# Outputs 4 to 7 of the first token pair by seven products, larger VectorE shares in that pair, and W1I of outputs 6 and 7 at place 15

## The chip, the cores and the metric

The kernel runs on one core of a Trainium2 chip. The metric is the device time of one execution in microseconds (us): 1032.77 us, the median of three runs (1032.61 to 1032.79). The engines are TensorE (PE; its weight loads are listed apart as PEld), VectorE (DVE), ScalarE (ACT), GpSimd (POOL) and SyncE (SP), which issues most DMAs.

## What is computed

An attention over channels is followed by two feed-forward layers, for N = 6016 tokens, C = 256 channels and FF = 2048 hidden units, all in float32:

```python
qn, kn = q / (norm(q, axis=1) + 1e-6), k / (norm(k, axis=1) + 1e-6)
a = softmax(kn.T @ qn / tau)                 # 256 x 256
x = v @ a                                    # tokens x 256
h = x @ w_in;  x = (h * sigmoid(1.702 * h)) @ w_out
h = x @ w2_in; out = (max(h, 0) + alpha * min(h, 0)) @ w2_out
```

## The kernel before

Precision: every float32 operand is kept as a high and a low half in a reduced type, and every product is three passes (high x high, high x low, low x high; `PASSES`, L41). One pass is one matmul of 128 x 128 weights with 512 columns of tokens. High halves are made by ScalarE (a copy), low halves by VectorE (a subtraction).

The attention is folded into the first layer: x @ w_in = v @ (a @ w_in), so a "W product" (`emit_w` L729, `emit_pair` L717) makes the weights WI from a and w_in, and ScalarE and VectorE put its high and low halves into WI. `emit_pair(4)` and `emit_pair(6)` each do it for two outputs, with 12 matmuls.

Tokens come in twelve chunks, and two chunks are a pair (`p`); a layer is `l`. The hidden units come in eight groups of 256, called outputs (`j`, 0 to 7), and FF tiles are 128 wide. For one output and one pair, the first matmul of a layer is a 2 x 2 by 2 x 2 block product (two channel halves, two FF tiles, two chunks).

- `direct` (L884) computes it as four blocks of two products each. It does so for the first `STRASSEN` outputs of the first pair.
- `quartet` (L906) computes it by seven products, for all others. It needs sums of the weight blocks (S2, S3, S4: `combine` L688, with steps "whole", four small sums, and the low half, and ScalarE's high half in between) and differences of the token blocks (T1 to T4: `prepare` L630). Its order on TensorE is A11, S1 x T1, A12 x B21, S2 x T2, S3 x T3, A22 x T4, S4 x B22. Between them stand the eight `outs.next()` of the output before: three matmuls each of the layer's second weights (WO) with the activated units, 24 in all. ScalarE copies the product of A11 into a second bank (L934), onto which A12 x B21 is added. Products S2 and S3 are copied by ScalarE (`copy`) and added by VectorE (`add` L849): u22 is the bank of S1 x T1 plus a copy, and S4 x B22 is then added onto that same bank for u12.

A unit is one activated 128 x 512 block: ScalarE does its activation and its high half, VectorE its low half (`low`, L878).

The order on every engine is written by the program at build time. VectorE's other work, whose results are needed later, is cut into steps of about 0.6 us, which `beside(time, ...)` (L750) issues between TensorE's products, up to a share `time` of step prices. There are two sources. `conv` (`Converter` L190) splits the weights w1i (pieces `ia[j]`) and w1o (`ob_[j]`) that have been loaded as 64-bit numbers: five steps ("shift", "power", "rest", "less", "low"), or, for j > 3, three steps, a sum that a DMA on POOL's queue does (`sent` L160), a copy by ScalarE and a split (L164). A piece is opened at the earliest three places after its load (`LOADING`), the copy of a landed sum is asked for three places after it was sent (`LANDING`), one per place. `bg` holds the steps of T1 to T4 and of the sums. What is due first is issued first; ties go to `conv`. ScalarE's part of a step waits in `put_off` and is issued at the start of a later `beside`. `finish` issues what is left of some steps, just before it is needed.

A place is one call of `beside` in pair 0: 0 to 4 x STRASSEN - 1 in `direct` (four per output), then three per quartet. `mid_way` (L1065) runs at each place of `direct` and issues W products and new steps by number of place. `FREE` (L31) and `FIRST` (L32) are the shares of quartets and of direct places.

Of the kernel before, what the change touches and what calls it, by code (L numbers as in the profile page):

```python
# [30 lines left out]
FREE = ((0.7, 2.8, 1.7), (0.0, 0.8, 0.8))  # L31
FIRST = 2.1  # L32
AHEAD = 2
QK_PARTS = [1, 3] + [4] * 9 + [2, 2, 2, 1]
TAIL = 12
LOADING = 3
LANDING = 3
STRASSEN = 6
ON_VECTOR = (4, 5, 6, 8)
# [20 lines left out]
def attention_then_two_ffns(ctx: ExitStack, tc: tile.TileContext, q, k, vT, tau, w1i, w1o, w2i, w2o, alpha, outT):  # L60
# [45 lines left out]
    class Convert:  # L106
# [4 lines left out]
        most = PIECE  # L111
# [78 lines left out]
    class Converter:  # L190


        STEPS = (("shift", 0.45), ("power", 0.45), ("rest", 0.63), ("less", 0.63), ("low", 0.63))
        ADDED = (("shift", 0.45), ("power", 0.45), ("rest", 0.63))

# [30 lines left out]
        def time(self, piece):  # L226
            if not piece or self.landed():
                return 0.63
            return self.list(piece)[self.at][1]
# [35 lines left out]
        def step(self):  # L265
# [5 lines left out]
            if not self.next() or self.landed():  # L271
                self.settle()
                return 0.63
            if not self.open:
# [34 lines left out]
        def due(self):  # L309
            return min(x.due for x in self.left())  # L310

# [19 lines left out]
    with tc.manual_schedule():  # L331
# [37 lines left out]
        LAST = 4 * STRASSEN  # L369
        PAIRS = {4: 13, 6: min(21, LAST - 2)}  # L370
        for j, x in ia.items():
# [258 lines left out]
        def prepare(l, p):  # L630
# [20 lines left out]
            def minus(nm, a, b):  # L651
# [4 lines left out]
                ("B11", B11), ("B21", B21), ("T1", None), ("T2", None), ("T3", None), ("T4", None), ("B22", B22))}  # L656
            D = 0.63
            early = [
# [18 lines left out]
            if (l, p) == (0, 0):  # L677
                def last():
                    ops["T4"] = operand()
                    tmp["T4"] = tmp["T2"]  # L680
                    minus("T4", B21, "T2")
                steps = [early[i] for i in (2, 3, 6, 7)] + [late[0], Step(D, None, last, hi["T4"])] + [late[i] for i in (4, 5)]
                for x, due in zip(steps, (4, 4, 4, 4, 3, 3, 3, 3)):
                    x.due = LAST - due
                return steps
            return early, late

        def combine(hi, lo, hi_s, lo_s):  # L688
# [20 lines left out]

            steps = [Step(0.63, None, whole, kind=1), Step(0.9, None, sums_, high, 1), Step(0.63, high, low, kind=1)]  # L710
            combining.append(steps)
# [172 lines left out]
        def direct(j, outs, mid_way):  # L884
# [3 lines left out]
            for i, (f, c) in enumerate((f, c) for f in range(2) for c in range(2)):  # L888
# [11 lines left out]
                mid_way(i)  # L900
                beside(FIRST, most=2 if (j, i) == (STRASSEN - 1, 3) else 3)
                u.low()
                units.append((f, c, u.pair))
            return Outs(0, 0, j, units)

        def quartet(l, p, j, outs, carry):  # L906
# [20 lines left out]
            ends = (l, p, j) == (1, NP - 1, NQ - 1)  # L927
            most = 1 if l else 2 if narrow else None
            u11, u22, u21, u12 = (Unit(l, 2 * j + f, c) for f, c in ((0, c0), (1, c1), (1, c0), (0, c1)))
            fork = (l, p, j) != (1, 0, 0)  # L930
            a, b = bank(), bank()
            product(a, j, A11, ops["B11"], n, True, True)
# [20 lines left out]
            if j != 1:  # L953
                beside(FREE[l][0], place=0, most=most)
            if fork:
# [11 lines left out]
            if before:  # L967
                b12.low()
            outs.next()
            product(a, j, S2, ops["T2"], n, False, True)  # L970
            u2 = copy(a)
# [5 lines left out]
            outs.next()  # L977
            beside(FREE[l][1], most=most)
            finish(late[:4])
            product(a, j, S3, ops["T3"], n, False, True)  # L980
            u3 = copy(a)
# [3 lines left out]
            evacuate()  # L985
            beside(FREE[l][2], most=most)
            finish(late)
            u22.act()
            product(a, j, A22, ops["T4"], n, False, True)
# [14 lines left out]
            return Outs(l, p, j, [(0, c0, u11.pair), (1, c1, u22.pair), (1, c0, u21.pair), (0, c1, u12.pair)])  # L1004

        operands[0, 0] = blocks
        conv.ahead = True
# [27 lines left out]
        small = [flat(G), Convert.pool.tile([P, T], F32, tag="top", name="second", bufs=3)]  # L1035
        sums0, pair1 = [], []
        outs, carry = None, []
# [21 lines left out]
        def combining_of(n):  # L1059
# [3 lines left out]
            bg.extend(combined[n])  # L1063

        def mid_way(i):  # L1065
            at = 4 * j + i
            if j < 3 and i == 1:
                if j == 0:
                    conv.need([ob_[0]])
                emit_w(j + 1)  # L1070
            for n, due in PAIRS.items():
                if at == due:
                    emit_pair(n)
                    for m in (n, n + 1):
                        if m >= STRASSEN:
                            combining_of(m)
            if j == 2 and i == 0:
                nc.sync.dma_start(alpha_sb, alpha)
            if at == LAST - 10:
                sums0.extend(prepare(0, 0))  # L1080
                bg.extend(sums0)
            if at == LAST - 2:
                combining_of(0)
            next_pair()

        for j in range(NQ):
            if j:
                conv.need([ob_[j - 1]])
            if j < STRASSEN:
                outs = direct(j, outs, mid_way)  # L1090
                continue
            finish(combined[j])
            finish(sums0)
            next_pair()
# [152 lines left out]
```

## Time and profile before

| | |
|---|---|
| median of three runs | 1032.77 us |
| the profiled execution | 1033.06 us |
| its span, first to last instruction | 1031.3 us |
| granted TensorE clock | 1.00 of full in the whole span |
| TensorE busy | 1025.7 us, 99% |
| VectorE busy | 750.5 us, 73% |
| ScalarE busy | 758.5 us, 74% |

A row of the timeline is: start, duration, engine, line, operation, tiles written <- tiles read, how many are merged, and in brackets the idle time of the engine before it and what ended it. A matmul's duration covers its way through the array; matmuls overlap, so their pace is read from their starts. Operations of VectorE and ScalarE overlap a little too: successors start about 0.5 to 0.6 us after one another.

### The profile page before, as it was taken

The page shows a single profiled execution, that of the slowest core. Times are in us where ns is not written, and L with a number is a line of the kernel's source. Part 1 is how long each engine was busy: PE and PEld are TensorE (multiplying, and loading weights), DVE is VectorE, ACT ScalarE, POOL GpSimd, SP SyncE. Part 2 cuts the span into 40 slices and gives each one's busy share as a digit, 9 for nine tenths or more (in the row PEclk, how much of TensorE's full clock was granted, in tenths as well). Part 3 has the DMA queues.
Part 4 walks back from the last instruction along what each step waited for, and adds up shares of the span by engine and source line. Part 5 has one row for each costly group of instructions (what it writes and reads, how often), then busy time and mean ns, then how long its engine had stood idle before and what let it go on. Part 6 is the DMA issues. An engine that isn't in the chain of part 4 may idle for free.

```text
span 1031.3 us, 12536 instructions
## 1 busy us (share of the span) xinstructions
PE 1025.7 (99%) x4634; PEld 865.4 (84%) x4634; DVE 750.5 (73%) x1226; ACT 758.5 (74%) x1273; POOL 38.4 (4%) x50
## 2 busy tenths in 40 slices
PE   9999999999999999999999999999999999999998
PEld 8888888888888888888998888888888888888997
DVE  4788888877778765445637877787877787877766
ACT  6787787778778766666767777777777777867776
POOL 4401000000000000000100000000000000000000
PEclk9999999999999999999999999999999999999999
DMA  9737222224325312003553001001001000000100
GB/s 356 266 106 178 65 74 70 98 80 168 114 89 179 113 41 77 1 1 132 196 168 113 1 21 62 1 21 62 1 21 62 1 18 25 36 0 1 41 1 36
DMA packets 32445, 79.72 MB, mean 77 GB/s; under 512 B 3200, under 2 KB 7808, under 8 KB 32384
## 3 DMA queue, kind: packets, MB, share of 16 engines
q1 hardware_dynamic: 28928, 65.29, 18.3%
q0 software_dynamic: 3456, 13.63, 4.6%
q8 instruction: 36, 0.59, 0.2%
q14 instruction: 25, 0.20, 0.1%
HBM read 52.96 MB, written 23.86 MB: 74 GB/s over the span
## 4 chain that ended last, share of the span: by engine, by line
PE 99%; DMA 0%; SPq 0%; ACT 0%; issue 0%
PE ps_o L814 50%; PE ps_h L785 44%; PE gram L433 4%; PE pw L567 1%; PE pw L723 1%; DMA qk<-in_k 0%; SPq L453 0%; PE nrm L510 0%; ACT s L831 0%; PE bc L532 0%; PE pt L555 0%
## 5 line engine op out<-in xcount | busy, mean ns | idle before, releaser
L814 PE MATMUL ps_o<-ghi,wo 128*128 128x512 f32 (+1 forms) x1536 | 561.0, 385 | 0.0
L785 PE MATMUL ps_h<-x,wi 128*128 128x512 f32 (+1 forms) x2034 | 548.1, 385 | 0.0
L785 PEld LDWEIGHTS ps_h<-x,wi 128*128 128x128 f32 x2034 | 381.2, 188 | 71.9 <-DVE wi L579 0.4
L814 PEld LDWEIGHTS ps_o<-ghi,wo 128*128 128x128 f32 x1536 | 288.4, 188 | 53.7
L814 PE MATMUL ps_o<-glo,wo 128*128 128x512 f32 (+1 forms) x768 | 296.1, 386 | 0.0
L851 DVE TENSOR_TENSOR g<-ps_h,s 128x512 f32<-128x512 f32 (+1 forms) x177 | 120.1, 679 | 103.9 <-PE ps_h L785 63.5
L880 DVE SCALAR_TENSOR_TENSOR glo<-g,sign_sb,ghi 128x512 fp32r<-128x512 f32 (+1 forms) x192 | 141.5, 737 | 55.4 <-ACT ghi L874 51.0
L923 ACT COPY s<-ps_h 128x512 f32<-128x512 f32 (+1 forms) x177 | 102.2, 577 | 106.4 <-PE ps_h L785 102.2
L882 DVE TENSOR_TENSOR glo<-g,ghi 128x512 fp32r<-128x512 f32 (+1 forms) x192 | 126.4, 677 | 65.9 <-ACT ghi L876 65.1
L814 PEld LDWEIGHTS ps_o<-glo,wo 128*128 128x128 f32 x768 | 144.2, 188 | 27.2 <-DVE glo L880 0.3
L874 ACT ACTIVATE ghi<-g,sign_sb 128x512 fp32r<-128x512 f32 (+1 forms) x192 | 137.2, 714 | 16.3 <-DVE g L870 10.9
L876 ACT CAST ghi<-g 128x512 fp32r<-128x512 f32 (+1 forms) x192 | 113.1, 612 | 3.4
L862 ACT ACTIVATE g<-ps_h 128x512 f32<-128x512 f32 (+1 forms) x108 | 63.3, 586 | 41.6 <-PE ps_h L785 41.1
L866 ACT ACTIVATE g<-g,sign_sb 128x512 f32<-128x512 f32 (+1 forms) x97 | 69.4, 716 | 29.2 <-DVE g L851 28.7
L870 DVE SCALAR_TENSOR_TENSOR g<-g,slope_sb 128x512 f32<-128x512 f32 (+1 forms) x97 | 71.6, 738 | 16.7 <-ACT g L866 16.6
L870 DVE SCALAR_TENSOR_TENSOR g<-ps_h,slope_sb,g 128x512 f32<-128x512 f32 (+1 forms) x95 | 69.7, 734 | 0.0
L934 ACT COPY ps_h<-ps_h 128x512 f32<-128x512 f32 (+1 forms) x89 | 50.2, 564 | 26.4 <-PE ps_h L785 26.1
L866 ACT ACTIVATE g<-ps_h,sign_sb 128x512 f32<-128x512 f32 (+1 forms) x95 | 64.3, 676 | 1.9 <-PE ps_h L785 0.2
L862 ACT ACTIVATE g<-g 128x512 f32<-128x512 f32 (+1 forms) x84 | 52.3, 622 | 13.8 <-DVE g L851 13.3
L433 PE MATMUL gram<-qk 128*128 128x256 f32 x156 | 34.3, 380 | 1.0 <-DMA qk<-in_k 1.0
L433 PEld LDWEIGHTS gram<-qk 128*128 128x128 f32 x156 | 29.4, 190 | 5.2 <-issue 1.4
L649 DVE TENSOR_TENSOR x<-t,x 128x512 fp32r<-128x512 f32 (+1 forms) x48 | 32.0, 674 | 0.0
(123 smaller groups left out, 493.5 us busy)
## 6 DMA issues: line engine op xcount, KB each, us to landing
wi<-w2i POOLq DMA_DIRECT2D x8, 896.0 KB, 4.9
xraw<-in_vT SPq DMA_DIRECT2D x10, 512.0 KB, 5.5
x<-ob SPq DMA_DIRECT2D x20, 256.0 KB, 2.9
xraw<-x SPq DMA_DIRECT2D x10, 512.0 KB, 3.7
out_T<-ob SPq DMA_DIRECT2D x20, 256.0 KB, 2.0
qk<-in_q SPq DMA_DIRECT2D x9, 512.0 KB, 10.3
qk<-in_k SPq DMA_DIRECT2D x9, 512.0 KB, 10.6
raw<-in_w1i SPq DMA_DIRECT2D x8, 512.0 KB, 5.0
```

What stands on the lines that cost most here:

```text
L433: nc.tensor.matmul(gram[m][:, :C], tiles[i][:, 1, r, m * P:(m + 1) * P], tiles[i][:, 0, r, :], start=(t == 0), stop=(t == R - 1))
L785: nc.tensor.matmul(ps[:, :n], WI[:, wq, a, blk], x[:, b, :n], start=(start and i == 0), stop=(stop and i == 2), skip_group_check=True)
L814: nc.tensor.matmul(acc_ps[c][d][:, :n], WO[:, j, a, f, d * P:(d + 1) * P], (hi, lo)[b][:, :n], start=(start and i == 0), stop=(stop and i ...
L851: nc.vector.tensor_tensor(self.src, ps[:, :self.n], s[:, :self.n], ALU.add)
L862: nc.scalar.activation(self.g, self.src, AF.Gelu_apprx_sigmoid)
L866: nc.scalar.activation(self.g, self.src, AF.Copy, scale=sign_sb[:, self.f])
L870: nc.vector.scalar_tensor_tensor(self.g, self.src, slope_sb[:, self.f], self.g, ALU.mult, ALU.max)
L874: nc.scalar.activation(self.hi, self.g, AF.Copy, scale=sign_sb[:, self.f])
L876: nc.scalar.copy(self.hi, self.g)
L880: nc.vector.scalar_tensor_tensor(self.lo, self.g, sign_sb[:, self.f], f32(self.hi), ALU.mult, ALU.subtract)
L882: nc.vector.tensor_tensor(self.lo, self.g, f32(self.hi), ALU.subtract)
L923: nc.scalar.copy(s[:, :n], ps[:, :n])
```

## The change

`STRASSEN` goes from 6 to 4, so outputs 4 and 5 of the first pair are quartets too. Their sums are combined within that pair instead of the next one. W1I of outputs 6 and 7 is multiplied at place 15 (before: 21), so w1i's pieces 6 and 7 are converted ahead of w1o's 3 and 4. T1 to T4 of the first pair are put on the list at place 7 (before: 14), and each is finished ahead of the product that needs it instead of all ahead of the first quartet. Shares grow: in quartets of this pair from 0.7, 2.8, 1.7 to 0.9, 3.1, 2.1, at three direct places by 0.5, after a pair's W product by 1.0. Step prices of 0.63 become 0.62. A piece of `conv` counts as due one place earlier, or four where a DMA does the sum.

```diff
+MORE = (0, 1), (1, 1), (2, 1)
-STRASSEN = 6
+STRASSEN = 4
...
         def due(self):
-            return min(x.due for x in self.left())
+            return min(x.due - (0 if x in self.flying else 4 if x.added else 1) for x in self.left())
...
         LAST = 4 * STRASSEN
-        PAIRS = {4: 13, 6: min(21, LAST - 2)}
+        PAIRS = {4: 13, 6: 15}
...
-                for x, due in zip(steps, (4, 4, 4, 4, 3, 3, 3, 3)):
-                    x.due = LAST - due
+                for x, due in zip(steps, (-1, 0, -1, 0, 1, 1, 1, 1)):
+                    x.due = LAST + due
...
-                beside(FIRST, most=2 if (j, i) == (STRASSEN - 1, 3) else 3)
+                beside(FIRST + (0.5 if (j, i) in MORE else 0), most=2 if (j, i) == (STRASSEN - 1, 3) else 3)
...
+        def operands_of(which):
+
+            finish([x for i, x in enumerate(sums0) if (0, 1, 0, 1, 2, 3, 2, 3)[i] <= which])
...
+            free = (0.9, 3.1, 2.1) if narrow else FREE[l]
...
+            if narrow:
+                operands_of(0)
...
-                beside(FREE[l][0], place=0, most=most)
+                beside(free[0], place=0, most=most)
...
+            if narrow:
+                operands_of(1)
             product(a, j, S2, ops["T2"], n, False, True)
...
-            beside(FREE[l][1], most=most)
+            beside(free[1], most=most)
             finish(late[:4])
+            if narrow:
+                operands_of(2)
             product(a, j, S3, ops["T3"], n, False, True)
...
-            beside(FREE[l][2], most=most)
+            beside(free[2], most=most)
             finish(late)
+            if narrow:
+                operands_of(3)
...
+        def pairs(at):
+            for n, due in PAIRS.items():
+                if at == due:
+                    emit_pair(n)
+                    spare[0] += 1.0
+                    for m in (n, n + 1):
+                        if m >= STRASSEN:
+                            combining_of(m)
+            if at == max(LAST - 1, PAIRS[6]):
+                combining_of(0)
...
-            if at == LAST - 10:
+            if at == 7:
                 sums0.extend(prepare(0, 0))
                 bg.extend(sums0)
-            if at == LAST - 2:
-                combining_of(0)
...
+            pairs(conv.now)
             finish(combined[j])
-            finish(sums0)
             next_pair()
             outs = quartet(0, 0, j, outs, carry)
```

(In `mid_way` the loop over `PAIRS` becomes a call of `pairs(at)`.)

## Rows read from the trace of the kernel before

**Rows 1.** The page: part 1 (busy time, share, instructions) and part 4 (the chain's shares).

```profile
PE 1025.7 (99%) x4634; PEld 865.4 (84%) x4634; DVE 750.5 (73%) x1226; ACT 758.5 (74%) x1273; POOL 38.4 (4%) x50
...
PE 99%; DMA 0%; SPq 0%; ACT 0%; issue 0%
```

**Rows 2.** TensorE's waits: who waited for whom, us in total, times, longest.

```profile
PE idle L391 <- POOL ones L384: 1.1, 1, 1.1
PE gram L433 <- DMA qk<-in_k: 1.0, 1, 1.0
```

**Rows 3.** TensorE's timeline at the W product of outputs 4 and 5.

```profile
88.21 0.62 PE L723 MATMUL pw<-wi_hi,eT_hi 128*128 128x512 f32 x2
...
90.94 0.85 PE L785 MATMUL ps_h<-x,wi 128*128 128x512 f32 x3
...
96.38 0.84 PE L785 MATMUL ps_h<-x,wi 128*128 128x512 f32 x3
```

**Rows 4.** Groups by line and form, TensorE: the full-width products of line 785.

```profile
L785 PE MATMUL ps_h<-x,wi 128*128 128x512 f32 x1698 | 464.8, 389 | 0.0
```

**Rows 5.** DMA issues: operation, count, size, median us to landing.

```profile
p<-top POOLq DMA_DIRECT2D x8, 256.0 KB, 4.9
```

**Rows 6.** Busy time in a stretch, of quartet 7: length, then PE, PEld, DVE, ACT, POOL.

```profile
131.20:141.40 10.20, 10.20 (x47) 8.45 (x46) 8.18 (x13) 7.26 (x14) 0.00 (x0) 1.00 0.00 0
```

**Rows 7.** VectorE's timeline behind the W product of outputs 4 and 5.

```profile
91.86 0.75 DVE L727 SCALAR_TENSOR_TENSOR wi<-pw,rs,wi 128x512 fp32r<-128x512 f32 x1 [0.62 <-ACT wi L726]
92.53 0.68 DVE L158 SCALAR_TENSOR_TENSOR p<-raw,p 128x512 f32<-128x512 uint32 x1
```

**Rows 8.** VectorE's timeline, the four sums of output 6.

```profile
117.87 0.29 DVE L699 TENSOR_TENSOR s<-t 128x128 f32<-128x128 f32 x1
...
118.61 0.28 DVE L702 TENSOR_TENSOR s<-t,s 128x128 f32<-128x128 f32 x1
```

**Rows 9.** ScalarE's timeline into the first quartet.

```profile
118.93 0.62 ACT L708 CAST wi<-s 128x512 fp32r<-128x512 f32 x1
...
121.56 1.14 ACT L645 CAST x<-xraw 128x512 fp32r<-128x512 f32 x2
122.60 0.58 ACT L934 COPY ps_h<-ps_h 128x512 f32<-128x512 f32 x1
```

**Rows 10.** TensorE's timeline, the first quartet (output 6): A11 and A12.

```profile
120.88 0.84 PE L785 MATMUL ps_h<-x,wi 128*128 128x512 f32 x3
...
123.60 0.84 PE L785 MATMUL ps_h<-x,wi 128*128 128x512 f32 x3
```

**Rows 11.** VectorE's timeline, pair 1, output 0.

```profile
146.16 0.69 DVE L882 TENSOR_TENSOR glo<-g,ghi 128x512 fp32r<-128x512 f32 x1 [1.51 <-ACT ghi L876]
146.77 0.68 DVE L649 TENSOR_TENSOR x<-t,x 128x512 fp32r<-128x512 f32 x1
...
149.64 0.68 DVE L851 TENSOR_TENSOR g<-ps_h,s 128x512 f32<-128x512 f32 x1
150.24 0.68 DVE L835 COPY ob<-ps_o 128x512 f32<-128x512 f32 x1
150.84 0.68 DVE L705 TENSOR_TENSOR wi<-s,wi 128x512 fp32r<-128x512 f32 x1
```

**Rows 12.** TensorE's timeline: S4 of quartet 7; S3 and A22 of pair 1, output 0.

```profile
140.60 1.52 PE L785 MATMUL ps_h<-x,wi 128*128 128x512 f32 x6
...
147.40 0.84 PE L785 MATMUL ps_h<-x,wi 128*128 128x512 f32 x3
...
149.44 0.84 PE L785 MATMUL ps_h<-x,wi 128*128 128x512 f32 x3
```

**Rows 13.** VectorE's timeline, quartet 7.

```profile
135.96 0.69 DVE L882 TENSOR_TENSOR glo<-g,ghi 128x512 fp32r<-128x512 f32 x1 [1.44 <-ACT ghi L876]
...
138.98 0.69 DVE L851 TENSOR_TENSOR g<-ps_h,second 128x512 f32<-128x512 f32 x1
...
141.48 0.69 DVE L851 TENSOR_TENSOR g<-ps_h,G 128x512 f32<-128x512 f32 x1 [0.49 <-PE ps_h L785]
```

More of the change, by code (lines that the diff above doesn't have):

```diff
@@ L190, in attention_then_two_ffns @@
     class Converter:
-        STEPS = (("shift", 0.45), ("power", 0.45), ("rest", 0.63), ("less", 0.63), ("low", 0.63))
-        ADDED = (("shift", 0.45), ("power", 0.45), ("rest", 0.63))
+        STEPS = (("shift", 0.45), ("power", 0.45), ("rest", 0.62), ("less", 0.62), ("low", 0.62))
+        ADDED = (("shift", 0.45), ("power", 0.45), ("rest", 0.62))
         def __init__(self):
@@ L227, in time @@
             if not piece or self.landed():
-                return 0.63
+                return 0.62
             return self.list(piece)[self.at][1]
@@ L272, in step @@
                 self.settle()
-                return 0.63
+                return 0.62
             if not self.open:
@@ L656, in prepare @@
                 ("B11", B11), ("B21", B21), ("T1", None), ("T2", None), ("T3", None), ("T4", None), ("B22", B22))}
-            D = 0.63
+            D = 0.62
             early = [
@@ L708, in high @@
                 nc.scalar.copy(hi_s(), box["s"])
-            steps = [Step(0.63, None, whole, kind=1), Step(0.9, None, sums_, high, 1), Step(0.63, high, low, kind=1)]
+            steps = [Step(0.62, None, whole, kind=1), Step(0.9, None, sums_, high, 1), Step(0.62, high, low, kind=1)]
             combining.append(steps)
@@ L1004, in quartet @@
             return Outs(l, p, j, [(0, c0, u11.pair), (1, c1, u22.pair), (1, c0, u21.pair), (0, c1, u12.pair)])
+        sums0 = []
         operands[0, 0] = blocks
@@ L1035, in attention_then_two_ffns @@
         small = [flat(G), Convert.pool.tile([P, T], F32, tag="top", name="second", bufs=3)]
-        sums0, pair1 = [], []
+        pair1 = []
         outs, carry = None, []
@@ L1070, in mid_way @@
                 emit_w(j + 1)
[L1071 to L1076, printed above, removed]
+                if j + 1 >= STRASSEN:
+                    combining_of(j + 1)
+            pairs(at)
             if j == 2 and i == 0:
                 nc.sync.dma_start(alpha_sb, alpha)
-            if at == LAST - 10:
+            if at == 7:
                 sums0.extend(prepare(0, 0))
                 bg.extend(sums0)
-            if at == LAST - 2:
-                combining_of(0)
             next_pair()
```

## The prediction

> **What bounds the kernel now.** I read the page's first and fourth part, then TensorE's waits, then TensorE's timeline around the code that changes. TensorE is busy for 99% of the span and the chain that ended last is TensorE for 99% [rows 1]. Its only waits are two at the very start, 1.1 and 1.0 us [rows 2]. A busy share says little of pipelined matmuls, so the pace is read from starts: from 90.94 to 96.38 us there are 24 matmuls of 512 columns, so 5.44 / 24 = 0.227 us each, back to back, and the twelve of pair 4's W product take 2.73 [rows 3]. So the kernel is the number of matmuls times 0.227 us; everything else is hidden. A change can win only by taking matmuls away, and loses whenever it makes one wait.
>
> The profiled execution took 1033.06 us (span 1031.3), 0.29 above the median of 1032.77. I work out differences in its span and put them on the median.
>
> **What is taken away.** Outputs 4 and 5 have been computed directly, 4 blocks x 2 products x 3 passes = 24 matmuls each; as quartets they take 7 x 3 = 21. That is 6 of the 1698 full-width ones of this line [rows 4]: 6 x 0.227 = 1.36 us, 0.13%. Nothing else of TensorE's count moves: W products, outs and W sums are only placed elsewhere. 1.36 us is the most that can be gained.
>
> The Trainium skill has two other prices for a matmul of 512 columns ("TensorE: Matmul & The Clock Gate", Back-to-back issue gap): about 216 ns alone and 131 ns in a stream with weight loads. By them the gain would be an estimated 1.29 or 0.79 us; the trace's 0.227 us, in just such a stream, decides.
>
> **What the plan then does.** I followed the planner's rules by hand, place by place (a place is 12 matmuls, 2.72 us), with the new shares, prices and due times. Tried on before, the same rules give the order that VectorE's rows show.
>
> Places 0 to 9: ia6 and ia7 (W1I of 6 and 7) now come ahead of ob3. ia4's last step of three falls at place 7, ia5's at 8, ia6's at 9, ia7's at 10. At 9, ia7's load is not three places old, so T1 and T2 of the first pair run there. Each landed sum is asked for three places later and one per place: ia4 is split at 10, ia5 at 11, ia6 at 13 and ia7 at 14. A sum on POOL's queue lands in 4.9 us [rows 5], under three places (8.2), so this costs nothing. Loads of W1I go ahead of W1O's on SP's queue, where only order changes.
>
> Place 13 (share 2.1 + 1.0): W product of 4 and 5, then split ia6, last step of ob3, three steps of ob4. Place 14 (2.1): split ia7, low T1, first step of sums 4 ("whole"); 0.24 is left, too little for the four sums (0.9). Place 15 (3.1): W product of 6 and 7, then the four sums of 4, low T2, T3, T4. The low half of sums 4 is left for `finish(combined[4])`, ahead of quartet 4.
>
> **Edits that cost nothing.** Outputs 4 and 5 as quartets bring ScalarE three copies each and VectorE two adds each; the quartet of output 7, which has them all, leaves ScalarE 2.9 us and VectorE 2.0 us idle of 10.20 [rows 6]. The larger shares add two steps per quartet, 1.2 us, which still fits into VectorE's 2.0. The cover is that idle time; where it's gone, the adds are late for TensorE, which is the last rival below. The second W product needs ia7's low half 0.45 us after its start: it starts at 90.94 + 5.44 = 96.38 [rows 3], so by 96.83. VectorE leaves the first W product at 92.53 [rows 7]; five steps (2.73), place 13's low (0.6) and the split (0.7) end at 96.5. It is hidden by 0.3 us; I put 0 and keep 0.5 for the range.
>
> **The first wait: quartet 4.** Set S = 96.38, the start of the second W product. VectorE's second half of it begins 3.65 us after the start and the next step 0.67 later (91.86 and 92.53 against 88.21) [rows 3, 7], so the sums of 4 begin at S + 4.32; they take 1.02 from the first start to the last end (117.87 to 118.61 + 0.28) [rows 8]: S + 5.34. ScalarE's high half of them is issued ahead of quartet 4's copy of the first product into the second bank (L934). ScalarE goes in order, so the copy waits behind it: high half 0.62 [rows 9], but successors start about 0.5 after a predecessor, so copy from S + 5.9 to S + 6.5. Before, that copy has nothing late ahead of it: at 122.60 it ends 0.4 before its user at 123.60 [rows 9, 10]. The user, A12 x B21, adds onto that bank, and stands 2.72 us behind the quartet's start (120.88 to 123.60) [rows 10], so at S + 2.73 + 2.72 = S + 5.45 if nothing waits. It waits 1.1 us. Behind it S2 x T2 wants the low half of sums 4 in its third pass: VectorE does low T2, T3, T4, place 15's low (4 x 0.6) and then this one, ending at S + 8.4; TensorE, 1.1 late, would want it at S + 8.4 less a weight load. Another 0.3. T3's low half comes 0.1 late behind that. Together 1.5 us, bounds 1.0 (copy alone, faster hand-over) and 2.0.
>
> Quartets 4 to 7: by the same rules the second share of 3.1 takes four steps of 0.62, not five, since 3.1 less four times 0.62 is a hair under 0.62 in floating point. Counted through: the last steps are low T2, split ob7 and T3 of pair 1. So T4 (two steps) of pair 1 is still open when pair 1 begins; before, only three low halves are.
>
> **The second wait: pair 1, output 0.** The share of 0.7 takes T4's first step, the next one T4's second, T3's low half and two steps of sums 1. T4's high half can only be put on ScalarE at the third share, so T4's low half follows there, behind u22's add and the evacuation: those start at 149.64 and 150.24, and the next step at 150.84 [rows 11], so T4's low ends at 151.5. A22 x T4 starts at 149.44 and wants it in its second pass, at 149.67 [rows 12]. Also T3's low now follows T4's second step (146.77 + 0.6 to 148.06) where S3 x T3 wants it at 147.63; this is inside the same wait. Together 151.5 - 149.67 + 0.06 = 1.9 us, bounds 1.4 and 2.4 (VectorE's u11 low, for which it waits on ScalarE until 146.16 [rows 11], is the fixed point from which it counts).
>
> **Sum.** -1.36 + 0 + 1.5 + 1.9 = +2.0 us: 1034.8. Its own range is 1033.8 to 1036.0.
>
> **The rivals.**
> One: T4 is ready (a step more is done in quartets 4 to 7, such as a fifth in one second share). Then there is only the first wait: -1.36 + 1.5 = +0.1, 1032.9. For it: one step more anywhere in 30 is enough. Against: the four shares leave 0.24 to 0.79 unused and nothing of 0.62 that isn't waiting fits.
> Two: neither wait, as the sums of 4 get in at place 14, or the copy isn't behind them: 1031.4. For it: VectorE has idle time all over pair 0 (2.0 us of quartet 7) [rows 6]. Against: at S the sums stand behind a W product whose end is fixed.
> Three, on the far side: VectorE's larger shares make u22's add late in each of quartets 4 to 7. S4 adds into the bank that u22 reads. In quartet 7 the add starts at 138.98 with four steps ahead of it [rows 13] and S4 at 140.60 [rows 12]; a fifth step makes it 139.6, done at 140.3, still 0.3 early. From there on it costs: where the share holds six, or the sums (1.02 us for a price of 0.9), it is about 0.6 a quartet, 2.4 us in all, on top of the two waits: 1037.2. Against: VectorE idles 1.44 us ahead of u11's low and 0.49 ahead of u12's add [rows 13], so a late quartet recovers in the next.
> That the change doesn't take the products away can't be: their number is fixed by the code.
>
> **How the numbers follow.** Both waits 0.42, first alone 0.20, neither 0.22, VectorE late as well 0.12; 0.04 for what I don't see. Predicted 1034.8. The range holds the first three: 1031.2 (no wait, 0.2 under) to 1036.1. About 0.2%, 2.07 us, is what a measurement of this kernel can tell from no change. Faster by that isn't reachable (1.36): 0.02. Both waits lie just at the upper bound (+2.0 against 2.07), so somewhat under half of them, 0.19, is slower, with 0.12 and 0.02 from the others: 0.33. Same: 0.65.
>
> **What would show it.** The count of 512-column matmuls of L785 falls by 6. Right: two gaps in TensorE's starts, one in quartet 4 ahead of A12 x B21, with ScalarE's high half of sums 4 and L934 just ahead of it, and one in pair 1's output 0 ahead of the second matmul of A22 x T4. A gap ahead of the second W product's third matmul would show ia7 late; gaps ahead of S4 in quartets 5 to 7 the third rival. A TensorE timeline without a gap, or a first wait under 0.8 us, proves the walk through the plan wrong.

## The result, and the profile after

The changed kernel takes 1038.9 us, the median of six runs (1038.09 to 1040.96), against 1032.78 of the kernel before (six runs, 1032.61 to 1032.94): a ratio of 1.0062, 95% interval 1.0052 to 1.0072. It is slower, by 6.1 us. The forecast was 1034.8 with a range of 1031.2 to 1036.1, so the time lies outside the range. The profiled execution took 1040.96 us with a span of 1038.9, 7.6 us longer than that of before. Ranges and ratios below leave out one run of five_direct, which took 1284.99 us at a mean granted clock of 0.753.

Page of the kernel after: part 1, the granted clock in 40 slices, part 4. The chain was 99% TensorE before [rows 1]; now VectorE and ScalarE stand in it.

```profile
PE 1029.9 (99%) x4628; PEld 866.0 (83%) x4628; DVE 751.8 (72%) x1230; ACT 761.7 (73%) x1279; POOL 38.3 (4%) x50
...
PEclk9999899999999999999999999999999999999999
...
PE 94%; DVE 3%; ACT 1%; DMA 1%; issue 0%; SPq 0%; DVEq 0%
```

The count fell from 4634 to 4628: the six matmuls are gone. The 99% busy share tells nothing, as before. TensorE's waits of the kernel after (line waited for, total, times, longest); none of these three was there before [rows 2]:

```profile
PE ps_h L786 <- ACT wi L709: 1.8, 1, 1.8
PE ps_h L786 <- DVE wi L706: 1.6, 1, 1.6
...
PE pw L724 <- ACT wi_hi L152: 0.6, 1, 0.6
```

TensorE's timeline of the kernel after, around the two W products and quartet 4. Waits are read from starts: where the next matmul starts more than 0.227 us after the last, the rest is lost. It answers [rows 3] and [rows 10].

```profile
87.56 0.39 PE L815 MATMUL ps_o<-ghi,wo 128*128 128x512 f32 x1
88.53 0.73 PE L724 MATMUL pw<-wi_hi,eT_hi 128*128 128x512 f32 x2 [0.58 <-ACT wi_hi L152]
...
97.11 0.62 PE L724 MATMUL pw<-wi_hi,eT_hi 128*128 128x512 f32 x2
...
99.84 0.85 PE L786 MATMUL ps_h<-x,wi 128*128 128x512 f32 x3
...
100.98 0.39 PE L815 MATMUL ps_o<-ghi,wo 128*128 128x512 f32 x1
103.16 0.73 PE L786 MATMUL ps_h<-x,wi 128*128 128x512 f32 x2 [1.78 <-ACT wi L709]
105.52 0.80 PE L786 MATMUL ps_h<-x,wi 128*128 128x512 f32 x1 [1.63 <-DVE wi L706]
106.11 0.63 PE L815 MATMUL ps_o<-ghi,wo 128*128 128x512 f32 x1
106.53 0.63 PE L815 MATMUL ps_o<-glo,wo 128*128 128x512 f32 x1
```

Three things are to be seen.

- **The first W product** should start at 87.79 and starts at 88.53: 0.74, and 0.38 more within it.
- **Quartet 4**: A11 starts at 99.84. The second product, S1 x T1, should start at 101.21 and starts at 103.16, 1.95 late. Its third pass, which takes the low half of the sums, should start 0.45 behind that and starts at 105.52, another 1.91. Together 3.85 (the last digits of the three starts make the 0.01).
- **Then the matmuls are slow**: 0.43 us from start to start instead of 0.227, until 111.5: 14 matmuls in 6 us, 2.9 lost.

Stretches of the kernel after: length, then busy time of PE, PEld, DVE, ACT, POOL with their counts, the granted clock, DMA share and GB/s. Between quartet 4's two waits TensorE is busy for 0.90 of 4.30 us, the granted clock is 0.91, and in the six microseconds that follow it is 0.50: TensorE's lower level, 1.2 GHz. By the 0.91 the clock fell some 0.8 us before the second wait ended (4.30 x 0.09 / 0.5).

```profile
97.00:101.20 4.20, 4.20 (x20) 3.27 (x18) 3.25 (x6) 2.23 (x4) 0.52 (x1) 1.00 0.81 191
101.20:105.50 4.30, 0.90 (x3) 0.30 (x2) 4.26 (x11) 2.32 (x4) 0.00 (x0) 0.91 0.15 22
105.50:111.50 6.00, 5.99 (x14) 4.74 (x15) 2.04 (x5) 1.25 (x3) 0.00 (x0) 0.50 0.42 159
```

VectorE is busy for 4.26 of the 4.30 us in which TensorE mostly stands still. Its timeline shows with what: it begins the second half of the second W product at 100.77, makes the four sums of output 4 (101.44 to 102.45), then T2's low half, the differences T3 and T4, the low half of an activated unit, and only then the low half of the sums, which it ends at 105.46.

```profile
100.77 0.75 DVE L728 SCALAR_TENSOR_TENSOR wi<-pw,rs,wi 128x512 fp32r<-128x512 f32 x1 [0.62 <-ACT wi L727]
101.44 0.28 DVE L700 TENSOR_TENSOR s<-t 128x128 f32<-128x128 f32 x1
...
102.17 0.28 DVE L703 TENSOR_TENSOR s<-t,s 128x128 f32<-128x128 f32 x1
102.37 0.68 DVE L650 TENSOR_TENSOR x<-t,x 128x512 fp32r<-128x512 f32 x1
...
104.78 0.68 DVE L706 TENSOR_TENSOR wi<-s,wi 128x512 fp32r<-128x512 f32 x1
```

ScalarE's timeline: ia5's copy (L152 at 87.87), for which the first W product waits, stands behind a copy of w1o's and behind a scaling that waits for its load; in quartet 4 the high half of the sums (102.48) can only follow VectorE's last sum, and the copy of A11 into the second bank (now L942) follows it at once.

```profile
86.48 0.62 ACT L152 CAST wo<-top 128x512 fp32r<-128x512 f32 x1
87.31 0.66 ACT L139 ACTIVATE p<-raw 128x512 f32<-128x512 f32 x1 [0.21 <-DMA raw<-in_w1o]
87.87 0.61 ACT L152 CAST wi_hi<-p 128x512 fp32r<-128x512 f32 x1
...
102.48 0.62 ACT L709 CAST wi<-s 128x512 fp32r<-128x512 f32 x1 [1.75 <-DVE s L703]
103.01 0.58 ACT L942 COPY ps_h<-ps_h 128x512 f32<-128x512 f32 x1
```

The rest is five short waits: 0.06 in S1 x T1 of quartet 5, and four of 0.29 to 0.33 us ahead of S4 x B22, such as this one in the first pair, where VectorE's add of u22 starts behind the four small sums. TensorE's timeline, then VectorE's:

```profile
136.43 0.39 PE L815 MATMUL ps_o<-ghi,wo 128*128 128x512 f32 x1
136.84 1.65 PE L786 MATMUL ps_h<-x,wi 128*128 128x512 f32 x6
```

```profile
135.90 0.28 DVE L703 TENSOR_TENSOR s<-t,s 128x128 f32<-128x128 f32 x1
136.10 0.68 DVE L852 TENSOR_TENSOR g<-ps_h,second 128x512 f32<-128x512 f32 x1
```

The account of the two profiled spans (1038.88 and 1031.30, a difference of 7.59), every wait being the distance of two starts less 0.227:

| | us |
|---|---|
| six matmuls fewer | -1.36 |
| the stretch ahead of the first matmul of L786 (49.92 against 50.34) | -0.41 |
| wait at the first W product | 1.12 |
| quartet 4: S1 x T1, then its third pass | 3.85 |
| 14 matmuls at the lower clock | 2.92 |
| five short waits | 1.26 |
| sum | 7.38 |

The 0.2 that is missing is spread over distances too small to single out.

### The profile page after: what moved, and what is told of

It is laid out like the page before. It is cut to its first block, busy times and chain, and to the rows that moved or that the text cites. A ratio compares the mean times of both kernels' runs of the same rounds, so it can differ in the third digit from the quotient of the medians.

```text
span 1038.9 us, 12534 instructions
## 1 busy us (share of the span) xinstructions
PE 1029.9 (99%) x4628; PEld 866.0 (83%) x4628; DVE 751.8 (72%) x1230; ACT 761.7 (73%) x1279; POOL 38.3 (4%) x50
## 4 chain that ended last, share of the span: by engine, by line
PE 94%; DVE 3%; ACT 1%; DMA 1%; issue 0%; SPq 0%; DVEq 0%
PE ps_o L815 47%; PE ps_h L786 41%; PE gram L434 4%; DMA raw<-in_w1o 1%; PE pw L724 1%; DMA qk<-in_k 0%; DVE glo L883 0%; DVE p L159 0%; DVE t L654 0%; ACT g L863 0%; ACT ghi L877 0%; DVE x L650 0%; DVE top L183 0%; PE pw L568 0%; DVE p L156 0%
## 5 line engine op out<-in xcount | busy, mean ns | idle before, releaser
L786 PE MATMUL ps_h<-x,wi 128*128 128x512 f32 (+1 forms) x2028 | 548.8, 387 | 3.5 <-ACT wi L709 1.8
L786 PEld LDWEIGHTS ps_h<-x,wi 128*128 128x128 f32 x2028 | 380.7, 188 | 77.9 <-DVE wi L706 2.3
L863 ACT ACTIVATE g<-ps_h 128x512 f32<-128x512 f32 (+1 forms) x104 | 60.7, 584 | 32.7 <-PE ps_h L786 31.7
L942 ACT COPY ps_h<-ps_h 128x512 f32<-128x512 f32 (+1 forms) x91 | 51.3, 564 | 26.5 <-PE ps_h L786 26.3
L863 ACT ACTIVATE g<-g 128x512 f32<-128x512 f32 (+1 forms) x88 | 54.9, 624 | 17.6 <-DVE g L852 17.3
```

Of the source, the lines that this page charges most:

```text
L786: nc.tensor.matmul(ps[:, :n], WI[:, wq, a, blk], x[:, b, :n], start=(start and i == 0), stop=(stop and i == 2), skip_group_check=True)
L863: nc.scalar.activation(self.g, self.src, AF.Gelu_apprx_sigmoid)
```

## The experiments

Two theories are tested. One: the second W product at place 15 stands directly ahead of quartet 4 and, with the conversion of ia6 and ia7 ahead of it, leaves VectorE no time for what quartet 4 needs. Two: single steps stand in the wrong place, so that each wait can be taken away by itself. Two was the theory of the first four runs; one took this form only behind them. A third was the rival of the prediction that VectorE's larger shares make TensorE's operands late. Times below are medians with the range of the runs; ratios are to the kernel before on the same chip. "Waits" is the sum over the profiled execution, taken from TensorE's starts as above.

**sums4_first.** The sums of output 4 come ahead of ia6 and ia7 in the list.

```diff
-            x.due = PAIRS[j - j % 2] if j > 3 else 4 * j - 3
+            x.due = PAIRS[j - j % 2] - j // 6 if j > 3 else 4 * j - 3
...
+            if n == STRASSEN:
+                for x, due in zip(combined[n], (13, 13, 14)):
+                    x.due = due
```

> The changed kernel with one thing else: the sums of output 4 are due at 13 and 14 (ahead of w1o's pieces), and W1I of 6 and 7 one place earlier, so that VectorE and ScalarE make the sums at places 13 and 14 instead of behind the second W product. My theory: the waits of quartet 4 (3.85 us ahead of and in S1 x T1) go to under 0.3, no stretch at half clock follows (2.9 us in the profiled run), and the wait of the first W product for the copy of ia5 (1.1 us) stays; so some 6.7 us less than the profiled run of the changed kernel, 4 to 5 less than its median: 1034 to 1035 us. Rival (VectorE is overloaded in the whole of pair 0, and the wait only moves): a wait of 2 us or more stands somewhere else in quartets 4 and 5, and the time stays above 1037.

Measured: 1040.88 us (1040.6 to 1041.98), ratio 1.0080 (1.0065 to 1.0095). The sums are there in time, and the lower clock is gone, but 1.88 us stay in quartet 4, now for T1's low half (the 1.6 of the first row), and waits of 0.3 to 2.0 us stand at seven places behind it: 8.8 us in all. TensorE's waits, three of nine rows:

```profile
PE ps_h L786 <- DVE x L650: 2.5, 3, 1.6
PE ps_h L786 <- ACT wi L709: 1.0, 1, 1.0
PE ps_h L786 <- DVE g L852: 0.6, 1, 0.6
```

So the wait is not a matter of that one step: another is late in its place, behind the second W product and two steps of w1o's conversion.

**ia5_copy_early.** Four put-off steps instead of three at the place where ia5's sum is due to be copied, so that the first W product doesn't wait.

```diff
-  most=2 if (j, i) == (STRASSEN - 1, 3) else 3)
+  most=2 if (j, i) == (STRASSEN - 1, 3) else 4 if (j, i) == (2, 2) else 3)
```

> The changed kernel with one thing else: at place 10 ScalarE may issue four put-off items instead of three, so the copy of ia4 is issued there and the copy of ia5 one place earlier. My theory: the wait of 1.1 us ahead of and in the W product of 4 and 5 goes, everything else stays (waits of 3.8 us in quartet 4, the clock's drop): 1.1 us less than the changed kernel on the same chip, about 1037.5. Rival (the copy waits for the DMA that sums, not for its place in the order): the wait stays at 0.7 or more and the time is that of the changed kernel.

Measured: 1042.44 us (1041.51 to 1043.03), ratio 1.0093 (1.0078 to 1.0108). The wait at the first W product goes, and the second W product waits 2.5 us for ia7's low half instead; quartet 4 still waits, 3.0 us by TensorE's starts against 3.85:

```profile
PE pw L724 <- DVE wi_lo L166: 2.5, 1, 2.5
PE ps_h L786 <- DVE wi L706: 1.6, 1, 1.6
PE ps_h L786 <- ACT wi L709: 1.0, 1, 1.0
```

VectorE does not lack time here: it stands idle for 3.15 us ahead of ia6's split. ScalarE's copy of ia6 now comes while the first W product still reads the pair's tile, of which there is one (`wi_tiles`), and waits for its end at 90.7. VectorE's timeline, then ScalarE's:

```profile
91.58 0.69 DVE L166 TENSOR_TENSOR wi_lo<-p,wi_hi 128x512 fp32r<-128x512 f32 x1 [3.15 <-ACT wi_hi L152]
```

```profile
90.92 0.62 ACT L152 CAST wi_hi<-p 128x512 fp32r<-128x512 f32 x1 [1.89 <-PE pw L724]
```

The lower clock is part of this time too: the granted clock is 0.50 from 101.0 to 104.0, behind the second W product's wait, and from 107.8 to 111.0, behind those of quartet 4.

**both_waits_off.** The two edits together.

> Both edits of the two runs before. My theory: the two waits and the half clock are all that costs; left are 1.36 us gained by six matmuls less and about 1.3 us of four or five short waits (0.3 each) ahead of S4 x B22: 1032.7, within 0.1% of the kernel before. Rival (VectorE overloaded): 1035 or more, with a wait of over 1 us in quartets 4 to 7.

Measured: 1043.6 us (1042.71 to 1044.64), ratio 1.0108 (1.0091 to 1.0125), waits 11.0 us: 3.1 at the second W product, 1.9 in quartet 4, 6.0 at seven places up to 293 us. The 3.1 comes again of 3.16 us in which VectorE stands idle for ia6's copy. Theory two falls for these two edits: runs with a mean granted clock of 0.999 or more take 1038.1 to 1038.3 us for the changed kernel, 1040.6 to 1042.0 for sums4_first and 1042.7 to 1042.8 here (these two on another chip, where the kernel before takes 0.2 us more than beside as_changed). Whether VectorE lacks time or the order of its steps is at fault isn't told apart by them.

**old_shares.** The changed kernel with the shares of before in the first pair's quartets.

```diff
-            free = (0.9, 3.1, 2.1) if narrow else FREE[l]
+            free = FREE[l]
```

> The changed kernel with the quartets' shares of before (0.7, 2.8, 1.7). Theory: the waits of quartet 4 and of the first W product stay, since they are made ahead of these shares; the short waits ahead of S4 in quartets 5 to 7 (0.06, 0.29 and 0.33 us) go or move: within 0.8 us of the changed kernel on the same chip. Rival (the larger shares are what makes VectorE late): 3 us or more faster than the changed kernel.

Measured: 1047.37 us (1046.97 to 1047.89), ratio 1.0141 (1.0126 to 1.0156), waits 15.0 us, 1.6 of them at the lower clock behind quartet 4's. The larger shares don't cause the loss, they hold it down, by 7.2 us against as_changed on the same chip; that it would be within 0.8 was wrong too.

**before_new_shares.** The other side of it: the kernel before, with the larger shares.

> The kernel before with one part of the change alone: the larger shares (0.9, 3.1, 2.1) in the two quartets of its first pair. Theory: with prices of 0.63 the second share still holds four steps of 0.63 and a shift; nothing waits, or one wait of 0.3 ahead of S4: 1032.6 to 1033.2, the same as before. Rival (larger shares make u22's add late as such): two waits and more, 0.6 us or over.

Measured: 1033.03 us (1032.66 to 1033.52), ratio 1.0002 (0.9993 to 1.0011), one wait of 0.08. By themselves, in two quartets and at prices of 0.63, they cost nothing that can be measured.

**wait_filled.** The changed kernel with 16 more matmuls, whose result is overwritten, ahead of S1 x T1 in quartet 4: 3.6 us of work put into the 3.85 that TensorE waits there.

```diff
             d = bank()
+            if narrow and j == STRASSEN:
+                for _ in range(16):
+                    nc.tensor.matmul(d[:, :n], WI[:, j, 0, A11], ops["B11"][:, 0, :n], start=True, stop=True, skip_group_check=True)
             product(d, j, S1, ops["T1"], n, True, True)
```

> The changed kernel with 16 matmuls of 512 columns more, ahead of S1 x T1 of quartet 4, into the bank that this product then overwrites (they change nothing that is computed; 16 x 0.227 = 3.6 us, just the length of the wait). My theory: the half clock behind the wait comes of TensorE standing still; filled, the granted clock stays 1.00 all through and the time falls by what the half clock cost, to 1037.9 to 1038.2 on any chip, although 16 matmuls more are done. Rival (the clock falls for another reason, or the time lost is all the wait): a stretch at 0.50 remains and the time is 1038.5 or more.

Measured: 1038.21 us (1037.85 to 1038.42), ratio 1.0052 (1.0037 to 1.0067). Sixteen matmuls more, and not slower. The mean granted clock of its four runs is 0.999 to 1.000. Stretches of this kernel, the same as above, now with work in the first of them; the granted clock stays at 1.00:

```profile
101.20:105.50 4.30, 4.24 (x19) 3.19 (x18) 4.23 (x11) 2.33 (x4) 0.00 (x0) 1.00 0.23 55
105.50:111.50 6.00, 6.00 (x28) 4.87 (x27) 3.54 (x7) 3.90 (x7) 0.00 (x0) 1.00 0.36 138
```

**as_changed.** The changed kernel itself, once more, on another chip.

> The changed kernel itself, beside the others on the same chip. It ran in 1038.1 to 1041.0 us with a granted clock of 0.997 to 0.999. Theory: its waits are fixed by the order of instructions and don't vary; what varies is how long the half clock holds behind the wait in quartet 4 (0 to 3 us). Rival: the waits themselves vary from chip to chip, which the profile would show.

Measured: 1040.17 us (1038.31 to 1040.23), ratio 1.0071 (1.0054 to 1.0088). The profiled execution is the one of 1038.31. It has waits in the same places (6.5 us, 3.96 of them in quartet 4; 0.93 at the first W product, 0.45 in S1 x T1 of quartet 5) and no lower clock behind them:

```profile
101.00:105.30 4.30, 0.89 (x4) 0.33 (x3) 4.27 (x11) 2.33 (x4) 0.00 (x0) 1.00 0.16 24
105.30:111.30 6.00, 6.00 (x26) 4.90 (x27) 3.51 (x7) 3.59 (x7) 0.00 (x0) 1.00 0.43 161
```

So the waits are nearly the same in both, as an order fixed at build time lets expect, and what the clock adds is 2.9 us in one profiled execution and nothing in the other. Of the ten runs of this kernel, the four with a mean granted clock of 0.999 took 1038.1 to 1038.3 us, the six at 0.997 and 0.998 took 1039.5 to 1041.0. The six runs after the change spread over 2.87 us (1038.09 to 1040.96), those with the wait filled over 0.57.

**place19.** Only the place: W1I of 6 and 7 at place 19, the first one of quartet 5, instead of 15. The due times of ia6 and ia7 follow from it, so the conversion moves with the product; the two aren't told apart.

```diff
-        PAIRS = {4: 13, 6: 15}
+        PAIRS = {4: 13, 6: 19}
```

> The changed kernel with the W product of outputs 6 and 7 at place 19 (ahead of quartet 5) instead of 15; their conversions are due later with it. Theory, mended after the first four runs: VectorE has too little time ahead of quartet 4, and what takes it is the conversion of w1i's pieces 6 and 7 and their W product, all ahead of quartet 4. Then the wait in quartet 4 and the one of the first W product go, with no stretch at half clock. In quartet 5, S1 x T1 waits some 0.6 us for the sums of 5, which stand behind the W product on VectorE and ScalarE, and about 1 us of short waits stays: 1033 us (1032.2 to 1034). Rival: four quartets' sums and T1 to T4 alone are too much (seven products for outputs 4 and 5 as such): the wait of quartet 4 stays at 1.5 us or more, the time over 1035.

Measured: 1034.21 us (1033.67 to 1034.34), ratio 1.0013 (1.0004 to 1.0023). Waits of 1.12 and 3.85 us and the lower clock are gone; 2.5 us are left, in seven waits of 0.28 to 0.62. The timelines of VectorE, ScalarE and TensorE of this kernel: the sums of output 4 begin at 93.92, their low half at 96.67, the high one at 94.98, all ahead of S1 x T1 at 97.41.

```profile
93.92 0.29 DVE L700 TENSOR_TENSOR s<-t 128x128 f32<-128x128 f32 x1
...
96.67 0.68 DVE L706 TENSOR_TENSOR wi<-s,wi 128x512 fp32r<-128x512 f32 x1
```

```profile
94.98 0.63 ACT L709 CAST wi<-s 128x512 fp32r<-128x512 f32 x1 [0.87 <-DVE s L703]
```

```profile
97.41 0.84 PE L786 MATMUL ps_h<-x,wi 128*128 128x512 f32 x3
```

This one number of the change is worth 4.7 us against 1038.9, and 6.0 against as_changed on the same chip. Theory one stands as far as the place goes.

**place19_sums_ahead.** In addition the sums of an output are finished ahead of a W product at the same place (the two calls change places).

> As place19, with the sums of 5 finished ahead of that W product instead of behind it. Theory: the 0.6 us wait in quartet 5 goes too: 1032.4 us (1031.6 to 1033.2), 0.4 to 0.7 under place19. Rival: the W product in between quartets is itself what TensorE waits for (banks, weights): the same time as place19 or more.

Measured: 1033.61 us (1033.29 to 1033.85), ratio 1.0008 (0.9999 to 1.0017): the wait of 0.62 is gone, 1.9 are left; 1.2 above what I expected, since I had put no price on those.

**sums_price.** In addition the step of the four small sums is priced 1.3 instead of 0.9, so that it doesn't stand ahead of u22's add.

> place19_sums_ahead with the four small sums priced at 1.3 instead of 0.9 (they take 0.94 to 1.02 us and start 0.1 late behind "whole", on which they depend). Theory: the short waits left (0.3 us each ahead of S4 x B22, at 129.6, 140.1, 211.8 and 283.6 us) come of shares that hold the sums and run over, so that u22's add is late; at the higher price they go, up to 1.2 us: 1032.4 us (1031.9 to 1033.2), under the kernel before. Rival: it is the number of steps ahead of the add, not the sums: the waits stay, 1033.4 to 1034.

Measured: 1035.17 us (1034.97 to 1035.98), ratio 1.0023 (1.0014 to 1.0033). The waits of 0.3 ahead of S4 go; 0.91 in quartet 4, 0.84 at 152 and 1.55 at 163 us come.

**old_prices.** place19_sums_ahead with steps of 0.63 again.

> place19_sums_ahead with step prices of 0.63 again instead of 0.62. Theory: at 0.63 one short step less fits ahead of u22's add in pairs 1 and 2, where the kernel before had no wait: the two waits at 211.8 and 283.6 us go, those of pair 0 stay; 0.6 us under place19_sums_ahead, 1033.0. Rival: the prices do nothing: 1033.6.

Measured: 1033.2 us (1033.01 to 1034.04), ratio 1.0005 (0.9995 to 1.0014), waits 1.65: those at 212 and 284 us go, one at 293 comes.

**five_direct.** STRASSEN 5 instead of 4, so only three matmuls fewer, with W1I of 6 and 7 at place 19.

> The changed kernel with five outputs directly (only 5, 6 and 7 by seven products) and the W product of 6 and 7 at place 19, its last direct place. Theory: the four places more give VectorE the time that it lacks; no wait ahead of the first quartet, 0.68 us gained by three matmuls less, about 1 us of short waits: 1033 (1032.2 to 1033.6). Rival: the first quartet meets the same wait wherever it stands (over 1.5 us): 1035 or more.

Measured: 1033.96 us, the median of all eleven, ten of them within 1033.63 to 1034.1; ratio 1.0010 (1.0001 to 1.0019). Half of the gain (0.68) and waits of 1.56: no better.

So far nothing beats the kernel before, and the question was whether the 1.36 us can be had at all. Four kernels on top of old_prices:

**less_second_share.** Fewer steps ahead of u22's add.

```diff
-            free = (0.9, 3.1, 2.1) if narrow else FREE[l]
+            free = (0.9 if j > STRASSEN else 0.0, 2.5, 2.8) if narrow else FREE[l]
```

> old_prices (place 19, sums ahead, prices of 0.63) with other shares in the first pair's quartets: 0.0, 2.5, 2.8 in quartet 4 and 0.9, 2.5, 2.8 in quartets 5 to 7, in place of 0.9, 3.1, 2.1. Fewer steps then stand ahead of u22's add, which follows the second share. Its kernel had short waits of 1.65 us in sum: 0.31 ahead of A12 and 0.39 at T3's low half in quartet 4, and 0.05, 0.29, 0.31 and 0.29 ahead of S4. Theory (the waits ahead of S4 are u22's add behind the second share's steps): they go, 0.31 and at most 0.39 stay, and the time is 1032.3 us (1032.0 to 1032.7), just under before. Rival (VectorE has no time to spare there, and the shortage only moves): waits elsewhere of as much, 1033.2 or more.

**three_steps.** 2.2 and 3.1 in place of 2.5 and 2.8.

> old_prices with shares 0.0, 2.2, 3.1 in quartet 4 and 0.9, 2.2, 3.1 in quartets 5 to 7: three steps in the second share, five in the third. Theory: nothing is left ahead of S4 either, 1032.3 us as less_second_share. Rival: five steps in the third share hold up the low halves behind it, and S2 or A12 of the next quartet waits by 0.3 us each time: 1033.2 or more.

Measured: 1033.9 us (1033.52 to 1034.33), ratio 1.0010 (1.0001 to 1.0019), and 1034.11 us (1033.58 to 1034.41), ratio 1.0012 (1.0003 to 1.0021). Waits of 2.2 each: in the first of them the waits ahead of S4 hardly shrink (0.29 and 0.31 to 0.25 and 0.24), and 0.81 comes behind the W product of 6 and 7, whose halves VectorE makes late. Both were expected at 1032.3; shares alone only move the shortage.

**copy_first.** less_second_share, and no put-off ScalarE step at the last place ahead of quartet 4: ia6's copy, and with it its split, comes one place later.

```diff
-  most=2 if (j, i) == (STRASSEN - 1, 3) else 3)
+  most=0 if (j, i) == (STRASSEN - 1, 3) else 3)
```

> less_second_share, and no put-off ScalarE step is taken at the last place ahead of quartet 4, so quartet 4's copy of the first product into the second bank (L934 before) has no copy of a landed sum ahead of it. Theory: the 0.31 us ahead of A12 x B21 in quartet 4 is that copy, and goes too: 1032.0 us (1031.7 to 1032.5). Rival: the put-off step comes one place later, its split with it, and a W product or a low half waits for that: as less_second_share or up to 1 us more.

Measured: 1032.62 us (1032.44 to 1033.83), ratio 1.0000 (0.9991 to 1.0009). The profiled execution, itself 0.67 above that median, has waits of 1.08: not only the wait for that copy went (0.29 in less_second_share), but also those of 0.81 and 0.25, as VectorE's steps behind it fall otherwise; 0.71 came at S3 x T3 of pair 1's output 0.

**copy_first_t3.** In addition one step more in the first share of quartet 7, so that one more low half of pair 1's differences is done in time.

```diff
-            free = (0.9 if j > STRASSEN else 0.0, 2.5, 2.8) if narrow else FREE[l]
+            free = (0.0 if j <= STRASSEN else 1.5 if j > 6 else 0.9, 2.5, 2.8) if narrow else FREE[l]
```

> copy_first with 1.5 in place of 0.9 for the first share of quartet 7 of the first pair, which brings one step more there, so that one low half more of pair 1's token differences is done before pair 1 begins. copy_first's kernel stood at 1032.62 us against 1032.89 with waits of 1.08 us: 0.71 at S3 x T3 of pair 1's output 0, 0.31 at 293 us, 0.05. Theory (each wait is a step in the wrong place, not a lack of VectorE time any more): the 0.71 goes to at most 0.1, the difference to before is -1.36 + 0.4 = -0.9 us or a little less, 1032.0 where before is at 1032.9, ratio 0.9991 (0.9987 to 0.9996). Rival (VectorE has nothing to spare): a wait of 0.5 us or more comes elsewhere, ratio 0.9997 or more.

Measured: 1032.03 us (1031.62 to 1032.28, eleven runs) against 1032.81 (1032.40 to 1033.38, fifteen runs), ratio 0.9991, interval 0.9982 to 1.0000. The 0.71 is gone and nothing has come in its place. The page, parts 1 and 4, of this kernel; both rows are like those of before [rows 1], with six matmuls fewer:

```profile
PE 1025.1 (99%) x4628; PEld 864.3 (84%) x4628; DVE 751.7 (73%) x1230; ACT 760.5 (74%) x1279; POOL 38.4 (4%) x50
...
PE 99%; DMA 1%; SPq 0%; ACT 0%; issue 0%
```

What is left of waits is 0.34 us (0.31 at 292 us). -1.36 + 0.34 is -1.02; measured are -0.78 between the medians and -0.93 between the profiled spans (1030.36 and 1031.30). Every run of it is under every run of before, though the interval just touches no change: a gain of 0.08%, about as small as this measurement can tell.

## Why the prediction was wrong

**What bounds the kernel, and the six matmuls: right.** 4628 instead of 4634, and wherever the waits are small the time follows -1.36 plus their sum: +0.29 against a measured +0.42 in old_prices, -1.02 against -0.78 in copy_first_t3.

**Second W product hidden by 0.3: right.** The split of ia7's sum ends at 97.27; the W product starts at 97.11 without a wait and wants it 0.45 later, at 97.56. The cover is as thin as forecast. VectorE, kernel after:

```profile
96.59 0.68 DVE L166 TENSOR_TENSOR wi_lo<-p,wi_hi 128x512 fp32r<-128x512 f32 x1
```

**The first wait, quartet 4: the step that failed.** The walk through the plan held to the hundredth: with S = 97.11 the four sums end at S + 5.34 (102.45), their high half at S + 5.99, the low one at S + 8.35; forecast were 5.34, the copy behind it from 5.9, and 8.4. What failed is who wants them first. The prediction has A12 x B21 wait for the bank, at S + 5.45, and S2 x T2 for the low half. But S1 lies in the slot of A21 (`S1 = A21`), and one of the four sums is written over it (the section on the kernel before names S2, S3 and S4 only), so S1 x T1, the second product, reads what the sums make: its high half at S + 4.09 and its low half, in the third pass, two matmuls later at S + 4.55. The low half's 8.35 asks for a wait of 8.35 - 4.55 = 3.8 in all; measured 3.85, against 1.5 forecast with an upper bound of 2.0. A wait is priced from its earliest reader, and the reader has to be looked up in the code by what it reads, not by its name.

**A wait that had no term: the first W product, 1.12 us.** The prediction has ia5's sum split at place 11. Two of the three put-off steps that ScalarE takes at place 10 are the high halves of T1 and T2, which the change brought there; ia4's copy goes to 11, ia5's to 12, and its split is at 88.51, where the W product wants to start at 87.79. In the kernel before the same split starts at 85.30, 2.9 us ahead of its W product at 88.21 [rows 3]. VectorE, kernel before, then kernel after:

```profile
85.30 0.69 DVE L165 TENSOR_TENSOR wi_lo<-p,wi_hi 128x512 fp32r<-128x512 f32 x1
```

```profile
88.51 0.69 DVE L166 TENSOR_TENSOR wi_lo<-p,wi_hi 128x512 fp32r<-128x512 f32 x1 [1.07 <-ACT wi_hi L152]
```

That this chain makes the wait is shown by ia5_copy_early: with a fourth put-off step at place 10 the wait is gone. The limit on put-off steps was left out of the walk for these pieces, and the end of that chain was not held against its reader as that of ia7 was.

**The lower clock: not foreseen, up to 2.9 us.** The prediction summed waits as if they cost only themselves. In the profiled execution TensorE stood still twice within 4.3 us and ran at 0.50 of its clock for the six behind it; as_changed shows nearly the same waits without it, and the mean clocks of 0.999 to 1.000 in all four runs of wait_filled make it likely that it needs them. The Trainium skill ("TensorE: Matmul & The Clock Gate", What's actually happening) says that the array's half rate is its state at rest, which activity lifts; the granted clock of 0.50 behind the two waits agrees with that. The same section of the Trainium skill says that the slow stretch at a kernel's start differs between runs of one kernel; here the stretch lies in the middle, and it differed as well, 0.50 and 1.00 behind nearly equal waits.

**The second wait, pair 1: 1.9 forecast, 0 measured.** So 1.9 us too much hid a part of what was forecast too low. The premise was that nothing fits into what the shares leave over. ob6's "shift", with a price of 0.45, did, in quartet 4's second share, and everything behind it moved up by a step. T4's second half and T3's low half are done in quartet 7, as rival one had it (VectorE, kernel after):

```profile
147.97 0.69 DVE L654 TENSOR_TENSOR t<-t,xraw 128x512 f32<-128x512 f32 x1
148.58 0.68 DVE L650 TENSOR_TENSOR x<-t,x 128x512 fp32r<-128x512 f32 x1
```

**Rival three, u22's add: right in kind.** It was priced at 0.6 a quartet where the four small sums stand ahead of the add; there were four such waits of 1.20 us together, two in the first pair and two, at 219 and 290 us, that come with the price of 0.62 (they go in old_prices). Its point of decision was right; its size, 2.4 us, was not reached.

**The range** ended at 1036.1 (the bounds of the two waits add up to 1035.8, not to the 1036.0 that the sum gives). By the prediction's own terms with the first reader put right (3.85 for 1.5) and T4 ready, the sum is +2.5; the wait at the first W product and the five short ones bring it to +4.9, the clock to +4.9 to 7.8. Measured: +5.3 to +8.2.

**What stays open:** whether ia6's and ia7's conversion or the W product itself at place 15 takes more of VectorE's time ahead of quartet 4, and how much of it is time and how much the order of the steps; and why a lower clock follows nearly equal waits in one execution and not in the other.

## What to carry to other kernels

When work is moved ahead of a deadline, list for each of its results the first instruction that reads it, by address and by pass, and compare the two times; a walk through the order that is exact to 0.1 us is worth nothing with the wrong reader. When one wait is taken away and the next comes up as long, as three times here, look whether the engine behind them is busy or waits itself: in ia5_copy_early it stood idle for 3.15 us behind a tile that was still being read. Moving a whole piece of work out of the stretch (place 19) did more here than tuning steps in it. Where TensorE stands still twice for some 2 us, count with a slow stretch behind it: six of ten runs of the changed kernel show a lower mean clock and 1.2 to 2.9 us more.

## What the runs showed of the hardware

- A wait of TensorE costs a little more than its releaser makes it late: in nearly all of them the second start behind it comes 0.11 us late as well. Two matmuls take 0.73 us behind a wait (at 88.53 and 103.16) and 0.62 in the stream (at 97.11). S4 and A11 behind the wait at 136.43 take 1.65 us for six matmuls, in the kernel before 1.52 [rows 12].
- The granted clock fell to 0.50 within the second of two waits of 1.8 and 1.6 us with two matmuls in between, and stayed there for the 6 us behind them, at a cost of 2.9 us, and didn't fall in another execution of the same kernel with waits of nearly the same length. With sixteen useless matmuls in the wait it stayed at 1.00, and the time was no longer (1038.21 against 1038.9).
